# Scaling the k and v sums of four batches on ScalarE in an attention and maxout kernel, with a new order of its pieces

## The chip, the core and the metric

The kernel runs on one core of one Trainium2 chip. The core has five engines with instruction queues of their own: TensorE (PE; PEld is its weight load, which overlaps the matmuls), VectorE (DVE), ScalarE (ACT), GpSimd (POOL) and SyncE (SP), and 16 DMA engines that they share. Each engine takes its instructions in the order in which the program gives them; across engines, semaphores order the work. The metric is the device time of one execution in microseconds. A profiled execution has its own time and a span, from its first to its last instruction; times within it are counted from the start of the span.

## The reference

Eight batches of eight heads with 576 positions of width 64, and 32 memory slots; then a feed-forward layer over 4608 tokens.

```python
a = softmax(phi, over the 32 slots)
k_m = einsum('bhsm,bhsd->bhmd', a, k)
v_m = einsum('bhsm,bhsd->bhmd', a, v)
attn = softmax(matmul(q, k_m.T) / 8)
x = matmul(attn, v_m)                    # heads side by side: 4608 x 512
h = maximum(maximum(x @ w1, x @ w2), x @ w3)
out = h @ w_out
```

Inputs and output are float32.

## The kernel before

The kernel goes batch by batch through small *pieces*. Which piece comes when is written out by hand: a string of words such as `F8@1!`, where the letter names the piece, the digit its part, the number behind `@` its batch. The loop at the end of the function issues them in this order, and as no scheduler stands behind it, each engine gets its instructions in the order of the words. A `!` sets the flag `swap`, which puts a piece's work on another engine than its usual one. A second string of digits gives the PSUM banks: each piece that needs one or two of the eight banks takes the next digit. A piece may start in a bank only when the earlier piece there has been read out.

The pieces that matter here, with their letters:

- `L`, `J`, `H`, `h`, `Y` are loads, all issued from GpSimd's queue (but phi of batch 0, from SP): of phi (`L0`), k (`L1`), v (`L2`), q (`L3` or two halves `J`), and the weights (`Y`). They cast to bfloat16 on the way, phi apart. Loads take their turn in one queue.
- `r` packs k beside a column of ones into the tile `kvr` (L105 on ScalarE with `!`, L107 on GpSimd). `E` is exp of phi, on ScalarE (L234).
- `B` (L256) is 72 small matmuls, of e against k, v and the ones, so that PSUM then holds the unscaled sums of k and v and the softmax denominator. `N` (`att_kv_norm`, L269 to L298) takes the reciprocal of the denominator and scales the sums to bfloat16 in `kvn`: one VectorE instruction for v (L280), and two for k (L291), one for each group of four heads. `K` (L306) transposes them on TensorE and copies the result (`kvt`). Batches 0 and 1 do this in two parts, k first (`N0`, `K0`), then v (`N1`, `K1`); the others in one (`N`, `K`).
- `Q` transposes q on VectorE; `S` (L342) is the scores, with two exponentials on ScalarE (L351). `a`, `s`, `c`, `m`, `X` normalise the attention on VectorE (`m` on GpSimd without `!`). Batches 0 and part of 1 use matmuls with ones (`M`, `R`) for it.
- `V` replaces w1 and w2 by w1 - w3 and w2 - w3, in place (on VectorE, on GpSimd with `!`), after batch 0's folds have read them. `D` (L453) *folds* v into the weights: matmuls of kvt with the weight, evacuated to bfloat16 (L177 on ScalarE or L181 on VectorE). So attention times v times weight becomes attention times a folded weight.
- `F` (`ffn1`, L504) is four matmuls of 288 columns; even parts are evacuated with a relu (L175 on ScalarE, L179 on VectorE), odd ones with a maximum on VectorE (L517) into the hidden tile `hx`.
- The output layer of batches 0 and 1 is `t` and `T` (`ffn2`): `t` opens a bank with four matmuls (L663), `T` ends it (L681, L690, L699 for the tile `T4` that two batches share) and copies 128 x 512 float32 into an `ot` tile. From batch 2 on, seven products `P` (L615) on sums and differences of blocks (`A` of activations, `U` of weights, on VectorE or GpSimd) take the place of eight; `P0`, `P1` and `P4` also copy a snapshot of their bank. `T4` stays for each pair of batches.
- `ot` tiles come from a pool of four. The four results of batch 0 are not stored at once: `g` (`send`, L719 to L721) issues such a store later, from ScalarE's queue, where it stands among ScalarE's instructions. All other stores but the last are issued from SP. An ot tile is given out again when its store has landed; the first to be free is taken first.
- `Z` is matmuls on zeros ahead of the first data.

Behind the first weights the pieces of neighbouring batches are mixed, so that evacuations, loads and matmuls overlap. `U` with batch 9 prepares sums of w_out in the space of `w3T`.

```python
SNAP = {0: "m5", 1: "m1", 4: "u2"}
opool = ctx.enter_context(tc.tile_pool(name="opool", bufs=4))
EVAC = {"D": "avaaa", "T": "vavav", "K": "v", "W": "vvv", "O": "aaaa", "F": "aaaaaa"}
```

`EVAC` gives the engine of each evacuation without `!` (a for ScalarE, v for VectorE) by part.

Of the kernel before, what the change touches and what calls it, by code (L numbers as in the profile page):

```python
# [15 lines left out]
def kernel(  # L16
# [126 lines left out]
    banks = iter(  # L143
        "".join(
            """
            00232204420145545045026402642602460246016042045026402462046064206402640230462064
            20642064206247042074204620460240640420402620420462046240724074204242020460246024
            602345040606426064026406416424126464642460263454342
            """.split()
        )  # L150
    )
# [114 lines left out]
                        tile_position=(HP * a, M * j),  # L266
                    )

    def att_kv_norm(b, part=None):  # L269
# [8 lines left out]
        if part != 0:
            v0 = 0 if part == 1 else D + 1
            nc.vector.tensor_tensor(  # L280
                out=kvn[:, 0].rearrange("p (a d) -> p a d", a=NG),
                in0=kvp[:, :, v0 : v0 + D],
                in1=rden.unsqueeze(2).to_broadcast([P, NG, D]),
                op=ALU.mult,
            )
        if part == 1:
            return
        k0 = D if part == 0 else 0
        for g in range(NG):
# [1 line left out]
            nc.vector.tensor_scalar_mul(  # L291
                out=kn.rearrange("p h (t d) -> p h t d", t=2),
                in0=kvp[:, g, k0 : k0 + D]
                .rearrange("p (d h) -> p h d", h=2)
                .unsqueeze(2)
                .to_broadcast([P, 2, 2, R]),
                scalar1=rden[:, g : g + 1],
            )  # L298
# [500 lines left out]


    for w in """
        E@0 h2@0 h3@0 h0@0 h1@0 L3@0 Z25@0 B0@0 Y2@0 I@0 N0@0 Z2@0 K0@0! Q0@0 Q1@0 Z9@0 S@0 Z2@0
        M0@0 M1@0 R0@0 R1@0 W0@0 Y3@0 W1@0 W2@0 Z6@0 O1@0 H3@0 O3@0 O2@0 H1@0 X1@0 B1@0
        X0@0 N1@0 K1@0 O0@0 Y0@0 D1@0! D0@0! D3@0 F8@0 Y1@0 F10@0! L0@1 L1@1 F6@0 J0@1
        F0@0! F2@0! D2@0 D4@0 F4@0 F1@0 F3@0 F5@0 F11@0 F7@0 V0@0! E@1 F9@0 B0@1 N0@1
        t2@0 T2@0! J1@1 Q0@1 L2@1 Q1@1 V2@0 K0@1! t1@0 T1@0 S@1 B1@1 V1@0 V3@0 L3@2 N1@1
        M1@1 a0@1 s0@1 R1@1 c0@1 K1@1 t3@0 T3@0 D2@1 m0@1! D0@1 X1@1 L1@2 X0@1 D1@1 Q0@2
        L0@2 t0@0 T0@0! L2@2 L1@3 Q1@2 L0@3 r0@2 F8@1! F4@1 F6@1! F7@1 E@2 F10@1! F2@1
        F5@1 F0@1 g2@0 B@2 D3@1 L2@3 L3@3 N@2 F9@1 F3@1 K@2! F11@1 g1@0 S@2 F1@1 D1@2!
        E@3 L1@4 U2@9 D0@2 D3@2 t3@1 T3@1 U0@9 T4@1! L0@4 r0@3 a@2 s@2 c@2 D2@2 B@3 L2@4  # L810
        m@2! U2@2 X@2 F10@2 N@3 F2@2 F11@2 F4@2 F0@2 K@3! L3@4 Q0@3 Q1@3 F6@2 F1@2 F8@2
        g0@0 F3@2 S@3 F7@2 a@3 F5@2 g3@0 s@3 F9@2 r0@4! E@4 U0@2 c@3 L0@5 U1@9 m@3! t2@1
        T2@1 X@3 U3@9 D0@3 D3@3 t0@1 T0@1! t1@1 T1@1 L1@5 D2@3 B@4 D1@3! N@4 P1@2! L2@5
        Q1@4 U1@2 F2@3 F6@3 F3@3 F8@3 L3@5 U3@2 L1@6 U0@3 A0@2! Q0@4 K@4! F4@3! F0@3
        F9@3 P2@2! A1@2! S@4 A2@2! A3@2! F5@3 E@5 a@4 P4@2 F1@3 r0@5 P0@2 L2@6 F10@3
        L0@6 s@4 F7@3 c@4 P5@2 m@4 D1@4! D3@4 U1@3 F11@3 P3@2 A0@3! D2@4 B@5 A2@3! N@5
        D0@4 X@4 T4@3! L1@7 A1@3! F10@4 Q0@5 K@5 F0@4 L3@6 Q1@5 P6@2! S@5 r0@6! F11@4
        F2@4! F1@4 L0@7 F6@4 F4@4! P1@3 F8@4 a@5 s@5 U2@3 D2@5 D3@5 c@5 P2@3! E@6 m@5
        A3@3! F5@4 P4@3 F3@4 F9@4 P0@3 D1@5! X@5 B@6 N@6 L2@7 D0@5 P5@3 U3@3 F8@5! F7@4
        P3@3! r0@7! L3@7 U0@4 F2@5! F10@5 E@7 U0@5 F3@5 Q0@6 A0@4! U1@4 P6@3 F11@5 F4@5  # L820
        Q1@6 F6@5 F9@5 K@6! F0@5 A2@4! U2@4 F5@5 S@6 F7@5 A1@4! a@6 A3@4! B@7 N@7 s@6
        D3@6 D1@6! P0@4 P1@4 U3@4 K@7! P2@4! F1@5 Q1@7 P4@4 c@6 D0@7 D1@7 D0@6 P3@4 P5@4
        U0@6 Q0@7 m@6 X@6 D2@6 D3@7 D2@7! A0@5! T4@5 S@7 A1@5! P6@4 F0@6 a@7 s@7 F4@6
        F10@6 F1@6 c@7 F2@6 U2@5 F6@6 P1@5 F3@6 F7@6 U1@5 P2@5 F8@6 A3@5! F9@6 F11@6
        P4@5 m@7 X@7 F5@6 P0@5! F6@7 F10@7! A2@5! F2@7 P3@5! F4@7! F0@7 P5@5 F8@7! F1@7
        F11@7 A0@6! U3@5 P6@5 F5@7 F9@7 U0@7 A1@6 U1@7 A2@6 F3@7 U1@6 P1@6 F7@7 P0@6
        P2@6! P4@6 U2@6 P1@7 A0@7 A3@6 U3@6 A1@7 U3@7! P2@7! P5@6! P3@6 U2@7! A2@7 A3@7
        P4@7 P6@6 P0@7! P5@7 P3@7! P6@7 T4@7!
    """.split():
# [32 lines left out]
```

## Time and profile before

| | us |
|---|---|
| median of 3 runs | 160.78 |
| range of the runs | 160.69 to 161.02 |
| the profiled execution | 160.41 |
| its span | 158.6 |

The profile is of one execution, with the TensorE clock granted in full (1.00). Its page lists busy times, the span in 40 slices, the DMA queues, the chain of work that ended last, the costliest groups of instructions by line, and DMA issues with their time to landing.

| stretch, us | length | PE busy | DVE | ACT | POOL | DMA share |
|---|---|---|---|---|---|---|
| 0 to 30 | 30.00 | 25.68 | 9.07 | 12.17 | 13.43 | 1.08 |
| 30 to 50 | 20.00 | 19.33 | 18.38 | 12.56 | 11.15 | 1.20 |
| 50 to 70 | 20.00 | 19.64 | 17.70 | 17.82 | 17.53 | 1.16 |
| 70 to 110 | 40.00 | 40.00 | 35.34 | 33.28 | 36.60 | 1.14 |
| 110 to 142 | 32.00 | 32.00 | 27.51 | 18.38 | 26.43 | 0.33 |
| 142 to 158.6 | 16.60 | 13.57 | 10.37 | 4.20 | 0.00 | 0.42 |

A group's line names the source line, engine, operation, the tiles and shapes, how often, the busy time and the mean in ns, then the idle time of the engine just before and what ended it. The lines of the chain and of the timeline begin with the start and the length in us. DMA shares of about 1.2 are the highest that the trace shows.

### The profile page before, as it was taken

How to read it: one execution, taken by the hardware profiler on the slowest of the kernel's cores; microseconds unless marked ns; L12 is line 12 of the kernel's file. 1: busy time of each engine (PE TensorE's matmuls, PEld its weight loads, DVE VectorE, ACT ScalarE, POOL GpSimd, SP SyncE). 2: the span in 40 equal slices, each digit the busy share in tenths (PEclk: the TensorE clock that was granted, in tenths of full speed). 3: DMA queues.
4: the chain of work that ended last, by engine and by line, in shares of the span. 5: the costliest groups of instructions: out<-in, count | busy, mean ns of one | idle time of the engine just before them, and what ended most of it. 6: DMA issues, size and time to landing. Idle time of an engine off the chain costs nothing.

```text
span 158.6 us, 5184 instructions
## 1 busy us (share of the span) xinstructions
PE 150.2 (95%) x2228; PEld 100.0 (63%) x2228; DVE 118.4 (75%) x205; ACT 98.4 (62%) x140; POOL 105.1 (66%) x100
## 2 busy tenths in 40 slices
PE   6996798999899999999999999999999999999992
PEld 2342544673456548646777577787874888888871
DVE  2032802789998997897998889899999868899851
ACT  4206335753787799997787789888976934124210
POOL 7960101993039959949969998999979996910000
PEclk9999999999999999999999999999999999999999
DMA  5999999999999999999999999999803500331544
GB/s 153 162 199 208 206 209 213 281 207 209 205 283 218 301 236 235 315 263 283 276 223 208 230 371 231 250 184 186 262 0 136 198 6 0 132 132 70 198 160 171
DMA packets 22934, 31.78 MB, mean 200 GB/s; under 512 B 1152, under 2 KB 18560, under 8 KB 22912
## 3 DMA queue, kind: packets, MB, share of 16 engines
q0 software_dynamic: 16128, 21.43, 71.3%
q1 hardware_dynamic: 6064, 8.85, 15.6%
q10 hardware_dynamic: 720, 1.18, 2.2%
q8 instruction: 17, 0.28, 0.7%
...
## 4 chain that ended last, share of the span: by engine, by line
PE 66%; DMA 23%; POOL 7%; issue 2%; ACT 1%; POOLq 0%
PE psum L504 24%; PE psum L615 24%; DMA w_sb<-in_moe_w_dram 14%; DMA kvr<-in_v_dram 10%; PE psum L453 4%; PE psum L681 4%; PE psum L256 3%; PE psum L663 2%; POOL ko L97 2%; PE psum L342 2%; POOL qq L112 1%; POOL kvr L97 1%; PE psum L690 1%; PE psum L699 1%; POOL w_sb L119 1%
## 5 line engine op out<-in xcount | busy, mean ns | idle before, releaser
L504 PE MATMUL psum<-hx,wp 128*128 128x288 bf16 x384 | 53.2, 286 | 0.1
L504 PEld LDWEIGHTS <-wp 128*128 128x128 bf16 x384 | 36.4, 98 | 11.7 <-issue 2.1
L517 DVE TENSOR_TENSOR hx<-psum,h 128x576 bf16<-128x576 f32 x48 | 34.9, 750 | 6.1 <-PE psum L504 5.0
L177 ACT CAST wp<-psum 128x1024 bf16<-128x1024 f32 (+1 forms) x29 | 27.5, 993 | 3.6 <-PE psum L453 3.4
L175 ACT ACTIVATE h<-psum 128x576 bf16<-128x576 f32 x34 | 21.5, 656 | 7.5 <-PE psum L504 6.8
L615 PEld LDWEIGHTS <-hx 128*128 128x128 bf16 x192 | 18.4, 98 | 3.5 <-issue 1.1
L164 PE MATMUL psum<-warm 128*128 128x512 bf16 x44 | 12.5, 440 | 1.2 <-DVE warm L131 1.2
L351 ACT ACTIVATE e<-psum 128x576 bf16<-128x576 f32 x16 | 9.5, 649 | 5.9 <-PE psum L342 5.9
L107 POOL COPY kvr<-ko 128x2304 bf16<-128x2304 bf16 x3 | 6.3, 2113 | 10.2 <-DMA ko<-in_k_dram 10.2
L615 PEld LDWEIGHTS <-w_sb 128*128 128x128 bf16 x120 | 11.6, 98 | 2.3 <-issue 0.7
L321 DVE STREAM_TRANSPOSE qT<-qq 128x576 f32<-128x576 f32 x16 | 11.8, 758 | 0.7 <-DMA qq<-in_q_dram 0.7
L629 ACT COPY snap<-psum 128x512 f32<-128x512 f32 x11 | 6.5, 595 | 8.7 <-PE psum L615 8.7
L540 POOL TENSOR_TENSOR w_sb<-hx 128x1024 bf16<-128x1024 bf16 x5 | 10.6, 2123 | 1.5 <-DVE hx L517 1.5
L218 POOL TENSOR_TENSOR w_sb<-w_sb 128x2048 bf16<-128x2048 bf16 x1 | 4.1, 4062 | 10.4 <-PE psum L453 10.4
L179 DVE TENSOR_SCALAR h<-psum 128x576 bf16<-128x576 f32 x14 | 10.3, 746 | 0.7 <-PE psum L504 0.6
L234 ACT ACTIVATE e<-ph 128x1152 bf16<-128x1152 f32 (+1 forms) x9 | 9.6, 1068 | 1.7 <-DMA ph<-in_phi_dram 1.6
L615 PE MATMUL psum<-wo_sb,hx 128*128 128x256 bf16 x72 | 9.8, 273 | 0.0
L615 PE MATMUL psum<-w3T,hx 128*128 128x256 bf16 x72 | 9.8, 273 | 0.0
L540 POOL TENSOR_TENSOR twb<-wp 128x256 bf16<-128x256 bf16 x11 | 7.4, 676 | 3.5 <-ACT wp L177 3.5
L177 ACT COPY ot<-psum 128x512 f32<-128x512 f32 x9 | 5.3, 595 | 7.0 <-PE psum L690 6.1
L647 DVE TENSOR_TENSOR ot<-psum,snap 128x512 f32<-128x512 f32 x12 | 8.2, 684 | 1.8 <-PE psum L615 1.1
L427 POOL TENSOR_TENSOR t<-t,sm 128x1152 bf16<-128x1152 bf16 x4 | 8.5, 2137 | 1.5 <-DVE sm L420 1.0
...
## 6 DMA issues: line engine op xcount, KB each, us to landing
...
qq<-in_q_dram POOLq DMA_DIRECT2D x7, 576.0 KB, 10.4
...
out_dram<-ot SPq DMA_DIRECT2D x14, 256.0 KB, 2.2
...
out_dram<-ot ACTq DMA_DIRECT2D x4, 256.0 KB, 6.7
```

Source lines behind the costliest of these rows:

```text
L164: nc.tensor.matmul(po[:, 0:BANK], lhsT=warm[:, 0:P], rhs=warm, start=True, stop=True)
L175: nc.scalar.activation(out=out_, in_=in_, func=AF.Relu)
L177: nc.scalar.copy(out=out_, in_=in_)
L179: nc.vector.tensor_scalar_max(out=out_, in0=in_, scalar1=0.0)
L234: nc.scalar.activation(out=s["e"][:, js], in_=loaded[b]["ph"][:, js], func=AF.Exp)
L321: nc.vector.transpose(out=s["qT"][:, j].rearrange("p j c r e -> p (j c r e)").bitcast(FP32), in_=loaded[b]["q"][:, j].rearrange("p j c d - ...
L351: nc.scalar.activation(out=e2[:, a].rearrange("p (t r c) -> p t r c", t=2, c=NC), in_=sc[a][:, :, 0:SH].rearrange("p t (c r) -> p t r c", ...
L427: (nc.vector if swap else nc.gpsimd).tensor_tensor(out=t, in0=t, in1=x.to_broadcast(list(t.shape)), op=ALU.mult,)
L504: nc.tensor.matmul(acc[:, h, 0:SH], lhsT=wps[b][:, g, w * DF + ft * P : w * DF + (ft + 1) * P], rhs=attn[:, g, c0 : c0 + SH], start=(g == ...
L517: nc.vector.tensor_tensor(out=hT[:, row(ft), (b % 2) * S : (b % 2 + 1) * S].rearrange("p (h n) -> p h n", h=2), in0=a, in1=s["h1", ft], op ...
L540: eng.tensor_tensor(out=out_, in0=in0, in1=in1, op=op)
L615: nc.tensor.matmul(po[:, q * CH : (q + 1) * CH], lhsT=lhs(k, q), rhs=rhs(k), start=(i < 3 and k == 0 and q == 0), stop=(k == KT and q == 1 ...
```

## The change

`att_kv_norm` gets the flag `swap`. With it, the scaling of v is two ScalarE multiplies (one for each group), and the two scalings of k are ScalarE multiplies too; the reciprocal stays on VectorE. In the new order `N` has the flag in batch 1 (both parts), 2, 5 and 6. The order of all pieces behind `Y1@0` is new, and so are the banks behind the first 30 digits; no piece is added or left out.

```diff
-    def att_kv_norm(b, part=None):
+    def att_kv_norm(b, swap, part=None):
...
         if part != 0:
             v0 = 0 if part == 1 else D + 1
-            nc.vector.tensor_tensor(
-                out=kvn[:, 0].rearrange("p (a d) -> p a d", a=NG),
-                in0=kvp[:, :, v0 : v0 + D],
-                in1=rden.unsqueeze(2).to_broadcast([P, NG, D]),
-                op=ALU.mult,
-            )
+            if swap:
+                for g in range(NG):
+                    nc.scalar.mul(
+                        kvn[:, 0, D * g : D * (g + 1)],
+                        kvp[:, g, v0 : v0 + D],
+                        rden[:, g : g + 1],
+                    )
+            else:
+                nc.vector.tensor_tensor(
...
+            (nc.scalar.mul if swap else nc.vector.tensor_scalar_mul)(
+                kn.rearrange("p h (t d) -> p h t d", t=2), k_, rden[:, g : g + 1]
             )
...
-            "N": lambda: att_kv_norm(b, i),
+            "N": lambda: att_kv_norm(b, swap, i),
...
-        X0@0 N1@0 K1@0 O0@0 Y0@0 D1@0! D0@0! D3@0 F8@0 Y1@0 F10@0! L0@1 L1@1 F6@0 J0@1
-        F0@0! F2@0! D2@0 D4@0 F4@0 F1@0 F3@0 F5@0 F11@0 F7@0 V0@0! E@1 F9@0 B0@1 N0@1
-        t2@0 T2@0! J1@1 Q0@1 L2@1 Q1@1 V2@0 K0@1! t1@0 T1@0 S@1 B1@1 V1@0 V3@0 L3@2 N1@1
-        M1@1 a0@1 s0@1 R1@1 c0@1 K1@1 t3@0 T3@0 D2@1 m0@1! D0@1 X1@1 L1@2 X0@1 D1@1 Q0@2
-        L0@2 t0@0 T0@0! L2@2 L1@3 Q1@2 L0@3 r0@2 F8@1! F4@1 F6@1! F7@1 E@2 F10@1! F2@1
-        F5@1 F0@1 g2@0 B@2 D3@1 L2@3 L3@3 N@2 F9@1 F3@1 K@2! F11@1 g1@0 S@2 F1@1 D1@2!
-        E@3 L1@4 U2@9 D0@2 D3@2 t3@1 T3@1 U0@9 T4@1! L0@4 r0@3 a@2 s@2 c@2 D2@2 B@3 L2@4
-        m@2! U2@2 X@2 F10@2 N@3 F2@2 F11@2 F4@2 F0@2 K@3! L3@4 Q0@3 Q1@3 F6@2 F1@2 F8@2
-        g0@0 F3@2 S@3 F7@2 a@3 F5@2 g3@0 s@3 F9@2 r0@4! E@4 U0@2 c@3 L0@5 U1@9 m@3! t2@1
...
+        X0@0 N1@0 K1@0 O0@0 Y0@0 D1@0! D0@0! D3@0 F8@0 Y1@0 L0@1 L1@1 F10@0! F4@0 F6@0
+        F2@0! D2@0 F0@0 J1@1 D4@0 F3@0 F1@0 F5@0 V1@0! E@1 F9@0 F7@0 F11@0 B0@1 J0@1
+        t3@0 L2@1 t1@0 N0@1! K0@1! Q1@1 T3@0 Q0@1 S@1 V3@0 V0@0 a0@1 U2@9! t2@0 s0@1
+        B1@1 N1@1! M1@1 L3@2 t0@0 c0@1 V2@0 m0@1! L1@2 R1@1 T2@0! X1@1 K1@1! Q0@2 T0@0!
+        X0@1 D1@1! D0@1! U0@9 T1@0 L0@2 D2@1 L2@2 Q1@2 F10@1! F8@1 F6@1 L0@3 F4@1! E@2
+        F9@1 r0@2 D3@1 F7@1 F0@1! F2@1 B@2 N@2! F11@1 E@3 F5@1 F3@1 F1@1 K@2! t1@1 S@2
+        L1@3 t3@1 g2@0 D1@2! L2@3 a@2 U1@9 g3@0 D2@2 s@2 D0@2 g0@0 c@2 L3@3 T3@1 U3@9
+        r0@3 m@2! X@2 T4@1! D3@2 B@3 N@3 T1@1 F0@2! L0@4 Q1@3 F6@2 F2@2 K@3 U2@2 U0@2
+        F8@2 F10@2 Q0@3 D3@3! S@3 F9@2 D1@3! D0@3 a@3 t0@1 s@3 c@3 L1@4 F7@2 g1@0 U1@2
+        L2@4 L3@4 L2@5 F4@2 U0@3 L0@5 r0@4! t2@1 F1@2 L1@5 F11@2 F3@2 E@4 m@3 T0@1! X@3
...
+        L2@6 D2@4 D3@4 P0@2! E@5 P5@2! F9@3 F7@3 P3@2 F1@3 m@4 F11@3 F5@3 r0@5! P6@2
```

Other flags change as well. The evacuations of `D1@1`, `D1@7` and `D2@7` go to ScalarE, those of `D0@1` and `D3@3` to VectorE; `T4@5` goes to ScalarE; of the even `F` parts one more is on VectorE; four more copies of `P` are on VectorE. `r0@5` goes from GpSimd to ScalarE. GpSimd takes `V1@0` in place of `V0@0`, and hands `A1@5`, `A0@6`, `U2@9` and `U1@5` to VectorE for `A2@6`, `U2@7` and `U3@7`.

More of the change, by code (lines that the diff above doesn't have):

```diff
@@ L145 @@
             """
-            00232204420145545045026402642602460246016042045026402462046064206402640230462064
-            20642064206247042074204620460240640420402620420462046240724074204242020460246024
-            602345040606426064026406416424126464642460263454342
+            00232204420145545045026402642642602460230064065606402640264062046234024604604602
+            46024620462502626024604250264262046262062460256025060252065260620026420642042616
+            241642442462106240620462646426402460426041624631120
             """.split()
@@ L279, in att_kv_norm @@
             v0 = 0 if part == 1 else D + 1
-            nc.vector.tensor_tensor(
-                out=kvn[:, 0].rearrange("p (a d) -> p a d", a=NG),
-                in0=kvp[:, :, v0 : v0 + D],
-                in1=rden.unsqueeze(2).to_broadcast([P, NG, D]),
-                op=ALU.mult,
-            )
+            if swap:
[7 more added lines that the diff above has]
+                nc.vector.tensor_tensor(
+                    out=kvn[:, 0].rearrange("p (a d) -> p a d", a=NG),
+                    in0=kvp[:, :, v0 : v0 + D],
+                    in1=rden.unsqueeze(2).to_broadcast([P, NG, D]),
+                    op=ALU.mult,
+                )
         if part == 1:
@@ L290, in att_kv_norm @@
             kn = kvn[:, 1:3, HP * g : HP * (g + 1)]
-            nc.vector.tensor_scalar_mul(
-                out=kn.rearrange("p h (t d) -> p h t d", t=2),
-                in0=kvp[:, g, k0 : k0 + D]
+            k_ = (
+                kvp[:, g, k0 : k0 + D]
                 .rearrange("p (d h) -> p h d", h=2)
                 .unsqueeze(2)
-                .to_broadcast([P, 2, 2, R]),
-                scalar1=rden[:, g : g + 1],
+                .to_broadcast([P, 2, 2, R])
+            )
+            (nc.scalar.mul if swap else nc.vector.tensor_scalar_mul)(
+                kn.rearrange("p h (t d) -> p h t d", t=2), k_, rden[:, g : g + 1]
             )
@@ L809 @@
-        F5@1 F0@1 g2@0 B@2 D3@1 L2@3 L3@3 N@2 F9@1 F3@1 K@2! F11@1 g1@0 S@2 F1@1 D1@2!
-        E@3 L1@4 U2@9 D0@2 D3@2 t3@1 T3@1 U0@9 T4@1! L0@4 r0@3 a@2 s@2 c@2 D2@2 B@3 L2@4
-        m@2! U2@2 X@2 F10@2 N@3 F2@2 F11@2 F4@2 F0@2 K@3! L3@4 Q0@3 Q1@3 F6@2 F1@2 F8@2
-        g0@0 F3@2 S@3 F7@2 a@3 F5@2 g3@0 s@3 F9@2 r0@4! E@4 U0@2 c@3 L0@5 U1@9 m@3! t2@1
-        T2@1 X@3 U3@9 D0@3 D3@3 t0@1 T0@1! t1@1 T1@1 L1@5 D2@3 B@4 D1@3! N@4 P1@2! L2@5
-        Q1@4 U1@2 F2@3 F6@3 F3@3 F8@3 L3@5 U3@2 L1@6 U0@3 A0@2! Q0@4 K@4! F4@3! F0@3
@@ L815 @@
[L815 to L826, printed above, removed]
@@ L827 @@
-        P2@6! P4@6 U2@6 P1@7 A0@7 A3@6 U3@6 A1@7 U3@7! P2@7! P5@6! P3@6 U2@7! A2@7 A3@7
-        P4@7 P6@6 P0@7! P5@7 P3@7! P6@7 T4@7!
+        X0@0 N1@0 K1@0 O0@0 Y0@0 D1@0! D0@0! D3@0 F8@0 Y1@0 L0@1 L1@1 F10@0! F4@0 F6@0
[3 more added lines that the diff above has]
+        X0@1 D1@1! D0@1! U0@9 T1@0 L0@2 D2@1 L2@2 Q1@2 F10@1! F8@1 F6@1 L0@3 F4@1! E@2
@@ new lines @@
+        F9@1 r0@2 D3@1 F7@1 F0@1! F2@1 B@2 N@2! F11@1 E@3 F5@1 F3@1 F1@1 K@2! t1@1 S@2
[3 more added lines that the diff above has]
+        L2@4 L3@4 L2@5 F4@2 U0@3 L0@5 r0@4! t2@1 F1@2 L1@5 F11@2 F3@2 E@4 m@3 T0@1! X@3
+        U1@3 F5@2 L3@5 T2@1 F4@3 D2@3 B@4 F6@3 N@4 F2@3! F0@3 K@4! U3@2 F10@3 A0@2! Q0@4
@@ new lines @@
+        L1@6 P1@2 Q1@4 A1@2! F3@3 S@4 P2@2! F8@3 A2@2! a@4 s@4 P4@2 A3@2! c@4 L0@6 D0@4
+        L2@6 D2@4 D3@4 P0@2! E@5 P5@2! F9@3 F7@3 P3@2 F1@3 m@4 F11@3 F5@3 r0@5! P6@2
+        U3@3 D1@4! B@5 X@4 N@5! P1@3 F8@4! Q1@5 F2@4 Q0@5 A0@3! F0@4 K@5! A1@3! L3@6
+        F10@4 F9@4 F6@4! P2@3 S@5 P4@3 L0@7 r0@6! F4@4! F7@4 A2@3! a@5 T4@3! D3@5 D1@5!
+        s@5 F11@4 c@5 A3@3! L1@7 U2@3 P0@3 F5@4 F3@4 E@6 F1@4 L2@7 P5@3! D0@5 B@6 Q1@6
+        D2@5 m@5 N@6! L3@7 X@5 P3@3! P6@3! F0@5! F10@5 F6@5 Q0@6 F2@5 K@6 F3@5 F8@5!
@@ new lines @@
+        F4@5 F5@5 E@7 P1@4! r0@7! A0@4! U2@4 F7@5 F1@5 U0@4 F9@5 P2@4 A1@4! U1@4 P4@4!
+        U0@5 A2@4! D3@6 B@7 D1@6! A3@4! U2@5 P0@4 N@7 Q0@7 U3@4 F11@5 S@6 Q1@7 A0@5!
+        P5@4 K@7! a@6 P3@4 s@6 S@7 P6@4 D0@7 D1@7! A1@5 U1@5! D0@6 P1@5! c@6 m@6! T4@5!
+        D2@7 A2@5! X@6 D3@7 D2@6 P2@5 P4@5 a@7 A3@5! U0@6 F8@6 F0@6! P0@5 F2@6 U3@5 s@7
+        F4@6! c@7 F9@6 m@7 P5@5 F10@6 F3@6 P3@5 X@7 F6@6 F5@6 F1@6 P6@5 U2@6 F11@6 F0@7
+        F7@6 F1@7 F8@7 A0@6 A1@6 U1@6 F2@7 F10@7 F6@7 A3@6 F3@7 F4@7! P1@6! F9@7 P2@6!
@@ L829 @@
+        U3@6 F5@7 P0@6! A2@6! U0@7 F7@7 P4@6 U1@7 F11@7 P3@6! U3@7 A0@7 P1@7 A1@7 P5@6!
+        P2@7 P4@7 U2@7 P6@6 A2@7 A3@7 P0@7 P5@7 P3@7 P6@7! T4@7
     """.split():
```

## The prediction

> **What bounds the kernel now.** I read the page's shares first, then stretches, then what TensorE waits for, then the chain.
>
> ```profile
> PE 150.2 (95%) x2228; PEld 100.0 (63%) x2228; DVE 118.4 (75%) x205; ACT 98.4 (62%) x140; POOL 105.1 (66%) x100
> DMA  5999999999999999999999999999803500331544
> 40.19:50.22 10.03, 9.72 (x148) 5.60 (x148) 9.64 (x18) 7.78 (x12) 4.18 (x4) 1.00 1.19 237
> 50.22:155.60 105.38, 105.20 (x1564) 76.56 (x1564) 90.70 (x149) 73.09 (x102) 80.34 (x65) 1.00 0.80 197
> PE psum L256 <- DMA kvr<-in_v_dram: 0.8, 2, 0.6
> 34.91 15.17 DMA kvr<-in_v_dram
> 50.08 0.14 issue
> 50.22 0.80 PE psum L256 x72
> 84.31 0.56 PE psum L453 x16
> 84.86 0.60 PE psum L504 x4
> ```
>
> The stretches give length, then busy time of PE, PEld, DVE, ACT, POOL, then clock, DMA share and rate. From 50.22 us to its last matmul TensorE idles 0.18 us, and the granted clock is 1.00. From 40 us on its only listed wait is for two loads of v; the second ends at 50.2, when the v of batch 2 has landed (issued at 34.91). So up to 50.2 us the loads set the time, afterwards TensorE's own work. The 3.0 us behind 155.6 are the last copy and its store. The last two lines price a change of matmul shape: two folds (0.23 us each, as at 51.02) take 0.56 and the ffn1 piece behind them 0.60 where others take 0.49: 0.21 us for each run of small-tile pieces.
>
> **The scaling itself.**
>
> ```profile
> L291 DVE TENSOR_SCALAR kvn<-psum,rden 128x128 bf16<-128x128 f32 x16 | 4.8, 344 | 0.1
> L280 DVE TENSOR_TENSOR kvn<-psum,rden 128x128 bf16<-128x128 f32 x8 | 2.3, 292 | 5.0 <-PE psum L256 4.8
> L312 ACT ACTIVATE kvtn<-psum 128x128 bf16<-128x128 bf16 x1 | 0.3, 278 | 1.0 <-DVE kvt L181 1.0
> ```
>
> Batches 1, 2, 5 and 6 move. VectorE loses 8 x 0.344 + 4 x 0.292 = 3.92 us. ScalarE gets 8 scalings of k and 8 of half a v; the nearest row is its one multiply from PSUM, 0.278. Bounds for 16: half of it (half a v is half as wide) and the 0.376 of its 128x256 copy, 2.2 to 6.0 us; I take 0.278, the nearest, for all: 4.4. For N@2 the latency is the reciprocal 0.165 plus 1.1 against 0.165 + 0.98 on VectorE. K@2 comes 2.07 us of ffn1 matmuls later (0.60 + 3 x 0.49): covered at both bounds (0.7 and 1.7). Cover gone, it would cost what exceeds 2.07.
>
> The Trainium skill speaks against this: "ScalarE: Activation LUTs", Rules for kernel authors, keeps multiplies on VectorE, and What ACT_TABLE_LOAD costs adds about 93 ns for a per-partition scale. By it an estimate is 16 x 0.37 = 5.9 us, still under K@2's cover; the rows here have ScalarE's multiply shorter than VectorE's (278 against 344), so neither changes the sum.
>
> The other flags: VectorE gets four more snapshot copies (+2.8), a combination, one ffn1 evacuation, V0 for V1 and small ones (+2.3) and loses a fold and a ffn2 evacuation (-1.9), in all about -0.7 us with the scaling. ScalarE gets the pack r0@5 (2.12), a fold (1.02), a ffn2 copy (0.6), loses four snapshots and a relu (-3.1) and small ones: about +5. GpSimd loses about 7. None of this is on TensorE's path by itself: totals stay under its 150.2. The tightest place: ScalarE between B1@1 and B@2 goes from 7.78 to some 10.3 us (its pieces added up by their rows, 2.5 more) of a stretch of 10.4.
>
> **The new order up to B@2.** GpSimd's early difference V1@0! is 128x1024 in place of V0's 128x2048 (4.06 us by L218, half: 2.1), so it issues J0@1 and v1 some 2.4 us sooner; the q and v of batch 1 and the loads of batch 2 keep their places and DMA is full (1.20), so v1 (31.95 + 8.2 = 40.15) and v2 (50.1) land as before. Worth nothing. L1@3 goes from 35.74 to behind r0@2, 48.1: v2 and ph3 fill the queue to some 51.8 meanwhile, k3 lands when ph3 did (36.48 + 18.3 = 54.8), and with r0@3's 2.1 is ready at 56.9, B@3 at 60. B1@1 has equal TensorE work ahead of it and waits for v1 still. Between it and B@2 the new order has D3@1 in addition (0.23, F9 for F5 is equal) and three runs of folds in place of one (2 x 0.21). Old: 9.71 busy of 10.03; new: 9.71 + 0.23 + 0.42 = 10.36, so B@2 starts at 40.19 + 10.36 = 50.55 and no longer waits. Behind it 0.23 us less is left, and the number of small runs is the same (18). Net +0.10.
>
> **The sends, moved past S@2 and the folds of batch 2.** The four results of batch 0 are stored from ScalarE's queue (g, L721), and the four ot buffers are then reused by T3@1, T4@1 and T1@1 in the order in which the sends free them: the built order makes these three copies, on ScalarE, wait for g2, g3 and g0.
>
> ```profile
> 50.00 0.38 ACTq L721 DMA_DIRECT2D out_dram<-ot  x1
> 52.54 0.34 ACTq L721 DMA_DIRECT2D out_dram<-ot  x1
> 58.47 1.13 ACT L177 COPY ot<-psum 128x512 f32<-128x512 f32 x2
> 65.24 0.34 ACTq L721 DMA_DIRECT2D out_dram<-ot  x1
> DMA to landing us min/median/max: 6.1/6.7/7.1
> out_dram<-ot SPq DMA_DIRECT2D x14, 256.0 KB, 2.2
> ```
>
> Before, g2 leaves at 50.00 and lands 6.7 us later, g1 at 52.54 and 6.1 later (58.64); T3@1 and T4@1 are copied from 58.47 and at 59.0. Nobody waits, with 0.4 us to spare. After, g2 stands behind both exponentials of S@2, g3 behind D1@2's cast, g0 behind D0@2's. TensorE from 50.55: B 0.75, F11 0.60, three F 1.47, K 0.17, t1 0.86, S 0.52 end S@2 at 54.92; t3 0.96, three folds 0.81, T3 0.97 end T3@1 at 57.66; T4 1.95, D3 and B@3 1.00, T1 0.97 bring F0@2 at 61.58. g2 can leave at 55.05 (65.24 is 0.08 behind the first exponential of S@3), g3 at 56.3, g0 at about 57.2. With 6.6 us to land: T3@1's copy, ready at 57.7, starts at 61.65; T4@1's at 62.9 (g3), ends 63.5; D3@2's cast, queued behind, ends 64.5; T1@1's copy at 65.1. Who waits: F0@2 takes T4@1's bank, so 63.55 in place of 61.58: 1.97 us. F6@2 takes D3@2's banks: from 64.04 to 64.55, 0.5. S@3 and D1@3 find ScalarE still catching up: 0.3 (relus at 0.65 spacing end 67.05 and 67.65, an exponential 68.3). Sum 2.8; with landings of 6.1 and 7.1, 2.3 and 3.3. VectorE and GpSimd idle meanwhile; nothing gives it back, as TensorE has no idle time left behind it.
>
> "DMA: Bandwidth & Descriptors", Anatomy of one DMA, of the Trainium skill fits a transfer by about 2.0 us plus its bytes at 436 GB/s (for GpSimd's path): 2.6 us here. By it g2 lands at 57.65, as T3@1's matmuls end, and the sum is +0.10. The quiet stores from SP agree (2.2); the four sends, under a DMA share above 1.1, do not (6.1 to 7.1), and at 55 to 63 us the queue of loads is as full.
>
> **Sum.** 0.10 + 2.8 = 2.9 on a span of 158.6, with 1.8 around it 163.3 for an execution like the profiled one (160.41). That one lies 0.4 under the median 160.78; from the median 163.6.
>
> **Rivals.**
> - *The sends land in time.* At the quiet row's 2.2 us g2 lands at 57.25 and g3 at 58.5, before T3@1 and T4@1 end: +0.10, 160.9. It decides below 2.6 us for g2 and 3.3 for g3. Against: all four sends. 0.13. (The page on DMA named above gives this case.)
> - *Faster*: VectorE, busy 9.64 of 10.03 before v2, is relieved and the late small waits go. But loads pin B@2: at most 0.23 + 0.18 are to be had, 160.4. 0.13.
> - *A dearer wait: the k of batch 4.* Its load moves from 49.55 to behind U2@2 and U0@2 on GpSimd (0.68 each), which wait for D3@2's cast: 64.5 + 1.4 = 65.9. The queue of loads is empty by some 63.2 (q3 at 48.81 + 12.7, then ph4). The shortest landing of such a load is 6.3: 72.2, then r0@4's 2.12 and E@4's 1.18: 75.5, B@4 due at 76.3. It decides from 7.1 us on; at 8.5 us 1.4 more, 165.0. 0.12.
> - *ScalarE's chain alone*: sends in time, but N@2, E@3 and K@2's copy (1.3 + 1.18 + 0.49 = 3.0 against 3.1 us of matmuls to S@2) run late by ScalarE's fullness, 0.4 to 1.0: 161.2 to 161.8. 0.08.
>
> **How the numbers follow.** Forecast 0.54, at 163.6, its own range 162.4 to 164.6 (landing 6.1 to 7.1, my clock of TensorE off by 0.4). What a measurement tells from no change is 0.2%, 0.32 us. Slower 0.54 + 0.12 + 0.08 = 0.74; same 0.13; faster 0.13. Eight in ten: from 160.8 (without the faster case and the lower half of the even one) to 165.0.
>
> **What would show it.** Right: ScalarE idle before two or three copies into ot at 58 to 63, ended by a store; TensorE idle some 2.5 us at 61 to 65, most before ffn1 matmuls of L513; stores from ScalarE's queue at 55 to 58 landing after 6 to 7 us. L282 and L305 near 0.28 us; TensorE's wait for v2 gone. Wrong: those stores landing in under 4 us, TensorE whole from 55 to 70, or a new wait at L256 for a load of batch 4 or 5.

## The result and the profile after

| | before | after |
|---|---|---|
| median, us | 160.74 | 167.04 |
| range of six runs each | 160.57 to 161.02 | 166.05 to 167.59 |
| ratio, 95% interval | | 1.0388 (1.0367 to 1.041) |
| the profiled execution | 160.41 | 167.59 |
| its span | 158.6 | 165.8 |

The change made the kernel 6.3 us slower. The prediction had the sign, but said 163.6, and the result lies above its range of 162.4 to 164.6. Ratios, here and below, compare the fast executions of two kernels; an execution over 1.5% above the fastest of its kernel is left out of them. The span grew by 7.2 us. The page's shares and the granted clock in the 40 slices first (4.1 us each):

```profile
PE 153.1 (92%) x2228; PEld 100.4 (61%) x2228; DVE 121.2 (73%) x197; ACT 102.3 (62%) x154; POOL 100.1 (60%) x98
...
PEclk9999999999999987999999999999999999999999
```

TensorE has the same 2228 matmuls and is busy 2.9 us longer; for part of that (1.55 us, below) the clock accounts, which is below full in the slices from 58 to 66 us. Of its waits these four bear on the change, as total, times, longest:

```profile
PE psum L690 <- ACT wp L177: 3.0, 1, 3.0
PE psum L513 <- DVE h L179: 1.1, 1, 1.1
PE psum L513 <- DVE hx L450: 0.7, 1, 0.7
PE psum L256 <- DMA kvr<-in_v_dram: 0.3, 1, 0.3
```

The first is new and large, the next two are new. The last was 0.8 us in two waits before; the one that is left is for the v of batch 1. As forecast, the v of batch 2 is no longer waited for, and B@2 starts at 50.41 us (forecast 50.55):

```profile
50.41 0.80 PE L256 MATMUL psum<-kvr,e 64*32 64x130 bf16 x72
```

ScalarE's timeline shows where the first comes from (start, length, engine; ACTq is an instruction that issues a DMA; in brackets the idle time before):

```profile
54.82 0.65 ACT L360 ACTIVATE e<-psum 128x576 bf16<-128x576 f32 x1 [0.86 <-PE psum L351]
54.87 4.50 ACTq L730 DMA_DIRECT2D out_dram<-ot  x1
...
59.41 1.01 ACT L177 CAST wp<-psum 128x1024 bf16<-128x1024 f32 x1 [3.40 <-issue]
...
62.54 0.58 ACT L177 COPY ot<-psum 128x512 f32<-128x512 f32 x1 [0.28 <-DMA out_dram<-ot]
```

The send g2@0 stands where the prediction has it, behind the exponentials of S@2, and starts at 54.87. But its *issue* takes 4.50 us, where the four issues of before took 0.34 to 0.38. ScalarE stands behind it for 3.40 us, then makes D1@2's cast. The ot buffer, the reason that the prediction gave, holds T3@1's copy for only 0.28 us. TensorE's timeline beside it:

```profile
60.48 2.39 PE L690 MATMUL psum<-wo_sb,hx 128*128 128x512 bf16 x6 [3.03 <-ACT wp L177]
62.80 1.06 PE L708 MATMUL psum<-wp,hx 128*64 128x512 bf16 x4
...
64.19 0.87 PE L256 MATMUL psum<-kvr,e 64*32 64x130 bf16 x72
```

T4@1 takes over the banks of D1@2 and waits 3.03 us for the cast. Then T4@1 and D3@2 are slow. From T4@1's start to B@3 it is 3.71 us; in the run with eight extra copies, below, the same pieces take 2.16 us (57.19 to 59.35). So 1.55 us more, and the stretches give the reason (length, busy PE, PEld, DVE, ACT, POOL, clock, DMA share, rate):

```profile
55.00:60.00 5.00, 2.44 (x32) 0.84 (x30) 3.85 (x4) 1.60 (x3) 2.27 (x2) 1.00 1.19 245
60.00:61.00 1.00, 0.53 (x3) 0.24 (x3) 0.79 (x2) 1.00 (x2) 0.00 (x0) 0.92 1.00 384
61.00:64.00 3.00, 3.00 (x17) 0.73 (x23) 0.00 (x0) 1.94 (x4) 0.00 (x0) 0.50 0.58 218
64.00:65.00 1.00, 1.00 (x81) 0.74 (x65) 0.00 (x0) 1.00 (x2) 0.00 (x0) 0.87 0.54 123
65.00:70.00 5.00, 4.94 (x79) 3.13 (x71) 4.21 (x9) 3.75 (x7) 4.40 (x7) 1.00 0.70 152
```

After the idle 3 us the granted clock is 0.50 for some 3.4 us (3.0, and the parts of a microsecond that 0.92 and 0.87 stand for). The other two waits, 0.7 us at 131 and 1.1 us at 148, stand behind pieces that VectorE did in 2.4 to 2.5 us. VectorE's timeline, with m@2 first for comparison, and GpSimd's at the times of the other two:

```profile
58.66 1.36 DVE L436 TENSOR_TENSOR t<-t,sm 128x1152 bf16<-128x1152 bf16 x1
...
128.50 2.37 DVE L436 TENSOR_TENSOR t<-t,sm 128x1152 bf16<-128x1152 bf16 x1
...
143.93 0.69 DVE L549 TENSOR_TENSOR w_sb<-w_sb,hx 128x1024 bf16<-128x1024 bf16 x1
144.66 2.49 DVE L549 TENSOR_TENSOR w_sb<-hx,w_sb 128x1024 bf16<-128x1024 bf16 x1
```

```profile
127.52 2.13 POOL L549 TENSOR_TENSOR w_sb<-hx,w_sb 128x1024 bf16<-128x1024 bf16 x1 [0.69 <-DVE w_sb L549]
129.60 1.78 POOL L549 TENSOR_TENSOR twb<-wp 128x256 bf16<-128x256 bf16 x1
...
144.04 2.56 POOL L549 TENSOR_TENSOR hx<-hx 128x1024 bf16<-128x1024 bf16 x1 [3.87 <-DVE w_sb L549]
```

The piece at 128.50 is m@6, which the new order's flags put on VectorE. (The list of other flags ahead of the prediction leaves this out: m@3 goes from VectorE to GpSimd, and m@6 the other way.) GpSimd is in the middle of an elementwise piece (to 129.65), and VectorE ends 1.2 us behind that: it looks as if the one waits for the other, then works at its own pace (alone, in batch 2, the same instruction takes 1.36). GpSimd's small twb (0.67 alone) then takes 1.78. The piece at 144.66 is A3@6 beside A2@6, which the flags put on GpSimd: 2.49 us in place of the 0.69 of the piece ahead of it. The Trainium skill says it so ("SBUF — State Buffer", Who interferes with whom): a VectorE instruction with two SBUF inputs and a GpSimd instruction that reads SBUF take turns on a shared pair of ports, and the second one waits whole. These rows agree to within 0.15 us.

The waits and the slow stretch add to 3.03 + 1.55 + 1.10 + 0.67 = 6.35 of the 7.2 us of span; the rest was not traced. The scalings themselves:

```profile
L305 ACT ACTIVATE kvn<-psum,rden 128x128 bf16<-128x128 f32 x8 | 2.5, 380 | 2.7 <-DVE rden L276 2.7
L282 ACT ACTIVATE kvn<-psum,rden 128x64 bf16<-128x64 f32 x8 | 2.1, 319 | 1.2 <-PE psum L256 0.8 <-DVE rden L276 0.4
```

Together 8 x 0.380 + 8 x 0.319 = 5.6 us as the durations go; neighbours overlap, so that ScalarE is busy with them for 2.5 + 2.1 = 4.6 us. No matmul waits for a scaling on ScalarE here.

### The profile page after: what moved, and what is told of

Its sections match the earlier page's. It is cut to its first block, busy times and chain, and to the rows that moved or that the text cites. A ratio compares the mean times of both kernels' runs of the same rounds, so it can differ in the third digit from the quotient of the medians.

```text
span 165.8 us, 5179 instructions
## 1 busy us (share of the span) xinstructions
PE 153.1 (92%) x2228; PEld 100.4 (61%) x2228; DVE 121.2 (73%) x197; ACT 102.3 (62%) x154; POOL 100.1 (60%) x98
## 5 line engine op out<-in xcount | busy, mean ns | idle before, releaser
L177 ACT CAST wp<-psum 128x1024 bf16<-128x1024 f32 (+1 forms) x30 | 28.4, 995 | 5.9 <-issue 3.4
L175 ACT ACTIVATE h<-psum 128x576 bf16<-128x576 f32 x33 | 20.3, 652 | 9.2 <-PE psum L513 8.1
L179 DVE TENSOR_SCALAR h<-psum 128x576 bf16<-128x576 f32 x15 | 11.3, 751 | 4.7 <-PE psum L513 3.2
L549 POOL TENSOR_TENSOR twb<-wp 128x256 bf16<-128x256 bf16 x12 | 9.5, 801 | 8.3 <-ACT wp L177 8.3
L549 POOL TENSOR_TENSOR hx<-hx 128x1024 bf16<-128x1024 bf16 x5 | 11.1, 2218 | 4.0 <-DVE w_sb L549 3.9
L690 PE MATMUL psum<-wo_sb,hx 128*128 128x512 bf16 x34 | 10.1, 412 | 3.0 <-ACT wp L177 3.0
L276 DVE RECIPROCAL rden<-psum 128x2 f32<-128x2 f32 x8 | 1.3, 158 | 14.0 <-PE psum L256 14.0
L638 ACT COPY snap<-psum 128x512 f32<-128x512 f32 x8 | 4.8, 597 | 10.2 <-PE psum L624 10.2
L549 POOL TENSOR_TENSOR w_sb<-hx 128x1024 bf16<-128x1024 bf16 x4 | 8.5, 2128 | 4.1 <-DVE hx L526 3.9
L107 POOL COPY kvr<-ko 128x2304 bf16<-128x2304 bf16 x2 | 4.2, 2104 | 11.1 <-DMA ko<-in_k_dram 11.1
```

Of the source, the lines that this page charges most:

```text
L175: nc.scalar.activation(out=out_, in_=in_, func=AF.Relu)
L177: nc.scalar.copy(out=out_, in_=in_)
L179: nc.vector.tensor_scalar_max(out=out_, in0=in_, scalar1=0.0)
L549: eng.tensor_tensor(out=out_, in0=in0, in1=in1, op=op)
L690: nc.tensor.matmul(po, lhsT=hT[:, row(fc), c0 : c0 + P], rhs=wo_sb[:, fc, :], start=(n == 0 and not early), stop=False,)
```

## The experiments

The theory formed from these traces has two parts. (A) g2@0 sits at a place of ScalarE's stream where its next instructions have to be fetched, and the issue waits for that. In the built program, which counts waits on semaphores as instructions, g2@0 is ScalarE's 67th (the 65th of those that the trace lists). One of the two queues that the page calls instruction queues moved a packet of 8 KB at 57.8 us (q14: 5 packets, 0.04 MB in all), and the issue ended at 59.37. (B) is the rival: the busy DMA queues held the issue. The prediction's own theory is the third. The collisions of VectorE and GpSimd are tried apart from these.

**shift8: eight small copies early on ScalarE.**

```diff
+            "j": lambda: [
+                nc.scalar.copy(out=idle_t[:, 8 * x : 8 * x + 8], in_=warm[:, 0:8])
+                for x in range(i)
+            ],
...
-        E@0 h2@0 h3@0 h0@0 h1@0 L3@0 Z25@0 B0@0 Y2@0 I@0 N0@0 Z2@0 K0@0! Q0@0 Q1@0 Z9@0 S@0 Z2@0
+        E@0 h2@0 h3@0 h0@0 h1@0 L3@0 Z25@0 B0@0 j8@0 Y2@0 I@0 N0@0 Z2@0 K0@0! Q0@0 Q1@0 Z9@0 S@0 Z2@0
```

> The kernel after, with eight 128x8 copies added to ScalarE in its idle time after the first sum of batch 0 (before 13 us), so that g2@0 is ScalarE's 75th instruction and not its 67th; nothing else changes its place. Theory A (the issue of g2@0 took 4.50 us because ScalarE's supply of instructions runs out at that place of its stream): the issue falls to 0.3 to 0.5 us, TensorE's 3.0 us wait and the halved clock behind it are gone, time 162.0 to 163.0 us; a shorter gap may show eight instructions earlier. Theory B (the issue was held by the state of the DMA queues at 54.9 us): it stays above 3 us and the time within 0.5 us of 167.0. My prediction's theory (the ot buffers come free late, the issue itself is short) also expects 167.0 here.

Measured: 165.87 us (165.15 to 167.0), ratio 1.0334 (1.0296 to 1.0372). ScalarE's timeline, then TensorE's:

```profile
54.78 0.38 ACTq L731 DMA_DIRECT2D out_dram<-ot  x1
...
61.39 0.59 ACT L177 COPY ot<-psum 128x512 f32<-128x512 f32 x1 [2.53 <-DMA out_dram<-ot]
```

```profile
57.19 1.46 PE L691 MATMUL psum<-wo_sb,hx 128*128 128x512 bf16 x6
...
59.35 0.83 PE L257 MATMUL psum<-kvr,e 64*32 64x130 bf16 x72
...
63.46 0.65 PE L514 MATMUL psum<-hx,wp 128*128 128x288 bf16 x4 [2.30 <-ACT ot L177]
```

The issue is back at 0.38 us at the same moment, 54.8, with the same loads under way: (A) holds and (B) falls. The 8 KB packet has moved with the eight instructions, from 57.8 to 52.9 us. But the time is not what (A) alone expected. With the issue short, the loss that was predicted comes to light: g2 lands 6.6 us after its issue, T3@1's copy starts at 61.39 (forecast 61.65), and F0@2 waits 2.30 us (forecast 1.97). In the kernel after, this wait hides behind the longer one. So each of the two theories had a part, and a loss was stacked behind a loss. Behind the 2.30 us the clock fell here as well, which (A) had not expected; here is one stretch, with the columns of the stretches above:

```profile
64.80:68.00 3.20, 3.20 (x17) 2.09 (x15) 1.90 (x4) 2.32 (x4) 3.18 (x6) 0.50 0.75 197
```

The profiled execution is the longest of the four, 167.0 us; the others, at a mean clock of 1.00, took 165.15 to 166.43.

**sends_from_sp: the four sends issued by SyncE.**

```diff
-        nc.scalar.dma_start(out=rows, in_=ot)
+        nc.sync.dma_start(out=rows, in_=ot)
```

> The kernel after, with all four sends of piece g issued by SyncE in place of ScalarE; ScalarE can no longer be held by an issue. The output rows and their order are the same. If only ScalarE's blocked queue cost the time (A or B): time 162.0 to 163.0 us. If the late freeing of the ot buffers costs it (the prediction's theory), TensorE still stands 2 to 3 us around 58 to 63 us and the time stays above 164.5 us. Under B the issue on SyncE is long as well (over 3 us) and T3@1's copy waits for the landing; under A it is below 1 us.

Measured: 164.48, 165.03, 167.41 and 167.54 us, ratio of the first two 1.0258 (1.0236 to 1.0281). The 162.0 to 163.0 us of (A) and (B) are missed. Issues are 0.36 to 0.46 us, and TensorE's wait at T4@1 is gone. But SyncE waits for nothing else there, so the sends left as soon as the results were there, the first at 44.0 us, and B@2 now waited 2.1 us for the v of batch 2. That mixes an earlier send with a freed ScalarE; the run says that the issue is short elsewhere, not what the place costs.

**sends_early: the sends ahead of B@2, on ScalarE.**

```diff
-        X0@1 D1@1! D0@1! U0@9 T1@0 L0@2 D2@1 L2@2 Q1@2 F10@1! F8@1 F6@1 L0@3 F4@1! E@2
-        F9@1 r0@2 D3@1 F7@1 F0@1! F2@1 B@2 N@2! F11@1 E@3 F5@1 F3@1 F1@1 K@2! t1@1 S@2
-        L1@3 t3@1 g2@0 D1@2! L2@3 a@2 U1@9 g3@0 D2@2 s@2 D0@2 g0@0 c@2 L3@3 T3@1 U3@9
+        X0@1 D1@1! D0@1! U0@9 T1@0 L0@2 D2@1 L2@2 Q1@2 F10@1! F8@1 F6@1 L0@3 F4@1! g2@0 E@2
+        F9@1 g3@0 r0@2 D3@1 F7@1 g0@0 F0@1! F2@1 B@2 N@2! F11@1 E@3 F5@1 F3@1 F1@1 K@2! t1@1 S@2
+        L1@3 t3@1 D1@2! L2@3 a@2 U1@9 D2@2 s@2 D0@2 c@2 L3@3 T3@1 U3@9
```

> The kernel after, with g2@0 moved behind F4@1, g3@0 behind F9@1 and g0@0 behind F7@1, ahead of B@2 as in the kernel before; all else in its place. Every theory that puts the loss on these sends expects TensorE's 3.0 us wait for D1@2's cast and the 1.65 us at the halved clock to go: 162.0 to 163.0 us. If the wait came from something else at 55 to 59 us on ScalarE (theory A without the send: whichever instruction is 67th now, the first exponential of batch 2, is held), a gap of 2 us or more stands at that instruction and the time stays above 164 us. What is left over the 160.7 of before should then be the 1.8 us of VectorE's and GpSimd's collisions at 129 and 145 us.

Measured: 163.72 us (163.25 to 164.15), ratio 1.0203 (1.0182 to 1.0223). The issues take 0.34 to 0.42 us; TensorE has no wait at T4@1 and none behind an ot copy, and the clock is 1.00. The instruction that is 67th now, a wait ahead of the first exponential, shows no gap: of what stood at that place in these runs, only an issue of a DMA suffered. Moving three words is worth 3.3 us of the 6.3. It is 0.7 over the forecast; a wait of 0.7 us for the v of batch 3 comes up at 60 us.

**scaling_alone: the kernel before, with only the scalings on ScalarE.** `att_kv_norm` is that of after, and N1@1, N@5 and N@6 get the flag in the same way as the two shown; order and banks are those of before.

```diff
-        F0@0! F2@0! D2@0 D4@0 F4@0 F1@0 F3@0 F5@0 F11@0 F7@0 V0@0! E@1 F9@0 B0@1 N0@1
+        F0@0! F2@0! D2@0 D4@0 F4@0 F1@0 F3@0 F5@0 F11@0 F7@0 V0@0! E@1 F9@0 B0@1 N0@1!
...
-        F5@1 F0@1 g2@0 B@2 D3@1 L2@3 L3@3 N@2 F9@1 F3@1 K@2! F11@1 g1@0 S@2 F1@1 D1@2!
+        F5@1 F0@1 g2@0 B@2 D3@1 L2@3 L3@3 N@2! F9@1 F3@1 K@2! F11@1 g1@0 S@2 F1@1 D1@2!
```

> The kernel before, in its own order and with its own banks, with the scalings of batches 1, 2, 5 and 6 moved from VectorE to ScalarE as in the kernel after. My prediction's step (covered on ScalarE, worth at most 0.1 us either way): 160.5 to 161.0 us. Rival (the four smaller ScalarE instructions hold the casts behind them, and TensorE waits): 161.2 to 162.5 us. If ScalarE's supply of instructions matters (A), a gap may appear near its 67th instruction, now the first cast after the exponentials of batch 2.

Measured: 162.52 us (162.2 to 163.07), ratio 1.0123 (1.0104 to 1.0141): 1.8 us slower. The prediction's step, 160.5 to 161.0, is missed: in the old order the scaling is not covered. ScalarE's timeline and then TensorE's at batch 2:

```profile
51.86 1.01 ACT L177 CAST wp<-psum 128x1024 bf16<-128x1024 f32 x1 [0.53 <-PE psum L462]
52.77 0.53 ACT L282 ACTIVATE kvn<-psum,rden 128x64 bf16<-128x64 f32 x2
53.18 0.64 ACT L305 ACTIVATE kvn<-psum,rden 128x128 bf16<-128x128 f32 x2
```

```profile
53.61 0.55 PE L315 MATMUL psum<-ident,kvn 128*128 128x128 bf16 x3 [0.72 <-ACT kvn L305]
```

The scalings stand behind the cast of a fold, and K@2 comes too soon. TensorE waits 1.0 us for scalings on ScalarE in this profile, 0.7 here and 0.3 at another K; how the other 0.8 us arise was not traced. The kernel after has no such wait: its order puts F11, F5, F3 and F1 between N@2 and K@2. So the new order does what it must for the scaling, and the time is lost elsewhere.

**early_swap_two: sends early, and m@6 and A2@6 back on the engines that they had.**

```diff
-        P5@4 K@7! a@6 P3@4 s@6 S@7 P6@4 D0@7 D1@7! A1@5 U1@5! D0@6 P1@5! c@6 m@6! T4@5!
+        P5@4 K@7! a@6 P3@4 s@6 S@7 P6@4 D0@7 D1@7! A1@5 U1@5! D0@6 P1@5! c@6 m@6 T4@5!
...
-        U3@6 F5@7 P0@6! A2@6! U0@7 F7@7 P4@6 U1@7 F11@7 P3@6! U3@7 A0@7 P1@7 A1@7 P5@6!
+        U3@6 F5@7 P0@6! A2@6 U0@7 F7@7 P4@6 U1@7 F11@7 P3@6! U3@7 A0@7 P1@7 A1@7 P5@6!
```

> The kernel with the sends early (163.72 us), with two late pieces given back to the engines that they had before the change: m@6 to GpSimd, A2@6 to VectorE. Theory: VectorE's L436 of batch 6 (2.36 us in place of 1.36) and its L549 of A3@6 (2.49 in place of 0.69) were long because GpSimd works on L549 pieces at the same time; TensorE's 1.1 us wait for h at 143 us and the 0.2 to 0.4 us at 127 us come from that. Then both are back at 1.4 and 0.7 us, the two waits are gone, and the time is 162.0 to 162.7 us. Rival (the long VectorE rows are hidden, or GpSimd is late with m@6 and X@6 waits for it in their place): 163.4 us or more, with a new TensorE wait at the pieces behind X@6.

Measured: 161.61 us (161.24 to 162.03, and one of nine at 164.57), ratio 1.0051 (1.0033 to 1.0069), 2.1 us less than with the sends early alone and a little below the forecast. The piece that took 2.49 us on VectorE, and m@6 on GpSimd:

```profile
140.36 0.69 DVE L549 TENSOR_TENSOR w_sb<-hx,w_sb 128x1024 bf16<-128x1024 bf16 x1
```

```profile
124.26 2.13 POOL L436 TENSOR_TENSOR t<-t,sm 128x1152 bf16<-128x1152 bf16 x1 [3.32 <-DVE sm L429]
```

Both waits of TensorE behind 120 us are gone, though m@6 takes longer on GpSimd (2.13) than it would alone on VectorE (1.36). VectorE's busy time is 117.0 us here, 121.2 in the kernel after.

**early_on_vector: sends early, all scalings on VectorE.** The flags of the five `N` are taken away.

> The kernel with the sends early (163.72 us), with all scalings on VectorE as before the change; the new order and banks stay. If ScalarE's scaling is worth its place in the new order (VectorE is short of time there), this is slower: 164.0 to 165.0 us. If it costs nothing and brings nothing (the prediction's step): 163.4 to 164.0 us. If the scaling itself is the loss, as 1.8 us were in the old order: 161.9 to 162.5 us.

Measured: 162.72, 164.10, 164.14, 164.98, 166.43 and 166.76 us; ratio of the first four 1.0202 (1.0156 to 1.0247), beside 1.0203 (1.0182 to 1.0223) with the scalings on ScalarE. In the new order the scaling's engine is worth nothing that these runs can tell, and with this interval they would not tell 0.5 us.

**before_shift13: the kernel before, with thirteen early copies.** The edit is that of shift8 with `j13@0`.

> The kernel before, with thirteen 128x8 copies added to ScalarE in its idle time before 13 us, so that its first send, g2@0, becomes ScalarE's 67th instruction, as it is in the kernel after; all else is unchanged. Theory A (a DMA issue at that place of ScalarE's stream waits for the refill): the issue that took 0.38 us takes 2 us or more, ScalarE's cast behind it is late by as much, and TensorE waits; time 162 to 166 us. Theory B (the DMA queues' state at 54.9 us in the kernel after): the issue stays below 0.5 us and the time within 0.4 us of 160.7.

Measured: 161.87 us (161.8 to 162.27), ratio 1.0076 (1.0049 to 1.0103).

```profile
49.70 3.12 ACTq L722 DMA_DIRECT2D out_dram<-ot  x1
52.86 1.01 ACT L177 CAST wp<-psum 128x1024 bf16<-128x1024 f32 x1 [2.52 <-PE psum L307]
```

The issue that took 0.38 us in the kernel before takes 3.12 once it is the 67th instruction: copies that cost nothing, 40 us earlier, make a store slow. The time is just below the expected 162 to 166, since TensorE has other work for part of it (it waits 1.3 us for the cast and 0.7 for a relu).

**shift2: two copies, so that g2@0 is the 69th.** The edit is that of shift8 with `j2@0`.

> The kernel after, with two copies added early, so that g2@0 is ScalarE's 69th instruction and the first exponential of batch 2 its 67th. Theory A1 (any issue that comes while the refill is under way waits for it): the issue of g2@0 is still over 2 us and the time 166 to 167.5 us. Theory A2 (only a DMA issue that stands exactly at the block's edge waits): the issue is below 0.5 us, and time and trace are those of the run with eight copies, 165.2 to 166.5 us, with the wait for the ot buffers at T3@1 of some 2.5 us.

Measured: 165.40, 166.41, 168.79 and 169.09 us. That is too wide to decide; the trace does.

```profile
54.80 2.90 ACTq L731 DMA_DIRECT2D out_dram<-ot  x1
```

A1, not A2: it need not be the very instruction. The three held issues ended 1.6 us after the 8 KB of instructions started to move: packet at 57.8 and end at 59.37 in the kernel after, 51.2 and 52.82 in before_shift13, 56.1 and 57.70 here. That the queue is ScalarE's shows in all thirteen traces: it moves 8 KB when ScalarE has started 65 to 70 of the instructions that the trace lists, and again at 189 to 193. So what the issue waits for comes with that packet; that it is the packet's landing is argued, as the trace shows no landing for it.

**k4_early: on top of early_swap_two, the load of batch 4's k earlier.** What early_swap_two's profile still shows is this wait of TensorE:

```profile
74.93 0.80 PE L256 MATMUL psum<-kvr,e 64*32 64x130 bf16 x72 [1.49 <-ACT e L234]
```

E@4 stands behind the pack of that k on ScalarE, and ScalarE stood 2.9 us for that k: the rival that the prediction called a dearer wait.

```diff
-        r0@3 m@2! X@2 T4@1! D3@2 B@3 N@3 T1@1 F0@2! L0@4 Q1@3 F6@2 F2@2 K@3 U2@2 U0@2
-        F8@2 F10@2 Q0@3 D3@3! S@3 F9@2 D1@3! D0@3 a@3 t0@1 s@3 c@3 L1@4 F7@2 g1@0 U1@2
+        r0@3 m@2! X@2 T4@1! D3@2 B@3 N@3 T1@1 F0@2! L0@4 L1@4 Q1@3 F6@2 F2@2 K@3 U2@2 U0@2
+        F8@2 F10@2 Q0@3 D3@3! S@3 F9@2 D1@3! D0@3 a@3 t0@1 s@3 c@3 F7@2 g1@0 U1@2
```

> The kernel with the sends early and the two late pieces given back (161.61 us), with the load of batch 4's k (L1@4) moved from behind t0@1, s@3 and c@3 to right behind L0@4, ahead of U2@2 and U0@2 on GpSimd's queue. Theory: what is left is TensorE's 1.5 us wait at B@4 (75 us) for E@4, which stands on ScalarE behind the pack of a k that landed 2.9 us late; the load is issued 2.5 us earlier, so most of that wait goes: 160.0 to 160.8 us. Rival (16 DMA engines are busy without a gap there, and a load that starts earlier pushes v and q of batch 3 back by as much): 161.3 us or more, with a new wait at B@3 or S@3.

Measured: 161.9 us (160.22 to 162.45, twelve runs), ratio 1.0051 (1.002 to 1.0083). The wait for E@4 is gone, and the time is the same: the forecast is missed, and the rival's time came without the wait for a load that it named. TensorE's timeline has this in its place:

```profile
65.37 0.30 PE L513 MATMUL psum<-hx,wp 128*128 128x288 bf16 x1
67.06 0.54 PE L513 MATMUL psum<-hx,wp 128*128 128x288 bf16 x3 [1.40 <-issue]
```

Between the first and second matmul of one piece TensorE stands, with nothing to wait for that the profile shows. TensorE's own packet of instructions (16 KB) started at 64.7. The same gap, of 0.49 and 2.31 us, is in the profiles of sends_early and early_on_vector (of which the second is the longest of its six executions):

```profile
66.51 0.54 PE L513 MATMUL psum<-hx,wp 128*128 128x288 bf16 x3 [0.49 <-issue]
```

```profile
68.08 0.53 PE L513 MATMUL psum<-hx,wp 128*128 128x288 bf16 x3 [2.31 <-issue]
```

There the packet started at 64.2 and 65.7, so that TensorE went on 2.3 to 2.4 us behind it each time. In early_swap_two it started at 62.0, and there is no gap. Why the packet comes late was not tried. Three of the twelve executions of k4_early took 160.22 to 160.92 us, near the forecast; the profiled one, at 162.21, is not among them, so whether they lacked the gap is open.

**k4_early_on_vector: the same with the scalings on VectorE.**

> The same with all scalings on VectorE, as before the change. If the scaling's engine is worth nothing once the order hides it (the prediction's step): within 0.4 us of the run beside it. If ScalarE's scaling is what lets the new order work: slower than it by 0.5 us or more, with waits for VectorE's h, hx or t.

Measured: 161.95 us (161.06 to 162.51, and one of twelve at 168.09), ratio 1.007 (1.0045 to 1.0095), beside 1.0051 (1.002 to 1.0083): the two can't be told apart. TensorE's gap is there too, 0.62 us, ending 2.3 us behind a packet at 64.4.

**after_swap_two: the kernel after with m@6 and A2@6 back, the sends where they are.** The edit is that of early_swap_two, alone.

> The kernel after, unchanged but for the same two late pieces (m@6 on GpSimd, A2@6 on VectorE); the sends stay where they are and the issue of 4.5 us with them. Theory: the collision of VectorE and GpSimd costs 1.8 to 2.1 us by itself, so 165.0 to 165.3 us. Rival (that loss hides behind the other one, or the gain seen with the sends early was the order of the loads): 166.3 us or more.

Measured: 165.22 us (164.76 to 165.58), 1.8 us less than the kernel after, as forecast. The collisions cost that by themselves, and their gain adds to that of the sends. The issue of g2@0 is held here too, a fourth time, and ends 1.55 us behind the packet (57.64):

```profile
54.91 4.28 ACTq L730 DMA_DIRECT2D out_dram<-ot  x1
```

## Why the prediction was right in sign and wrong in size

The 6.3 us, from medians: the three sends at their new place 3.3 to 3.6 (after to sends_early, after_swap_two to early_swap_two), the two pieces with exchanged engines 1.8 to 2.1, and what is left over before in early_swap_two, 0.9.

- *What bounds the kernel* held: behind B@2 TensorE has no slack, and the stalls there counted.
- *The scaling itself*: covered, as said; on either engine the time is the same in two pairs of runs, within their intervals. The term was right in size where it counts: ScalarE is busy 4.6 us with the scalings for 4.4 forecast, though each alone takes longer (0.319 and 0.380) than the 0.278 taken for it. The sum of the durations is 5.6 us; the estimate by the page "ScalarE: Activation LUTs", What ACT_TABLE_LOAD costs, of the Trainium skill, 5.9, is near that. The old order did not cover it (1.8 us).
- *The sentence that failed most is "None of this is on TensorE's path by itself: totals stay under its 150.2".* Totals of busy time say nothing about which pieces run beside which. VectorE's total was to fall by about 0.7 us and rose by 2.8, from 118.4 to 121.2. Two exchanged pieces set VectorE and GpSimd against each other on long elementwise work from SBUF, and m@6 and A3@6 took 1.0 and 1.8 us more. TensorE had no slack there and waited 0.7 and 1.1 us. This is 1.8 to 2.1 us that the sum did not have.
- *The new order up to B@2*: right, 50.41 against 50.55, and no wait for v2.
- *The sends, moved past S@2 and the folds of batch 2*: 2.8 us forecast, 3.3 to 3.6 measured. The place and the engine were right; TensorE waits at T4@1 and not, as forecast, at F0@2. The step that failed is "g2 can leave at 55.05", with the 0.34 to 0.38 us of an issue taken from rows of before: an issue was treated as having one price. It took 4.50 us and blocked the casts behind it; then the clock was halved, which no step had. That 2.8 lies near the measured size is luck: the wait in the kernel after is for a cast behind the issue, and not for ot buffers. The chain of late ot buffers that the prediction worked out exists, and with the issue short it came out nearly as written (2.30 us for 1.97, landing 6.6 us for 6.6). In the kernel after, it is hidden. By medians, that chain (shift8 against sends_early) costs about 2.1 us of the 2.8 forecast, and the long issue adds about 1.2. The landing of 2.6 us by "DMA: Bandwidth & Descriptors", Anatomy of one DMA, of the Trainium skill is not borne out there: 6.6 us in shift8, 3.7 at the least for a send of batch 0 in the kernel after.
- *Rivals*: "the sends land in time" and "faster" are out. "ScalarE's chain alone" is out in the new order. "A dearer wait: the k of batch 4" did not show in the kernel after, where the earlier stall probably gave that load time, but stands as 1.5 us in early_swap_two's profile, once the other losses are taken away. It was weighed as an alternative to the forecast, where it can stand behind it; but the run without that wait was no faster.

That these parts add to 6.3 us is no proof by itself: each path goes in steps from the kernel after to early_swap_two and from there to the kernel before. What the last 0.9 us consist of stays open, as the run without the wait for the k of batch 4 did not win them back. No version tried beats the kernel before: the best ones are at 1.005.
